# Reading two scalar inputs late instead of first: a one-core attention and gated-MLP kernel on Trainium2

## The chip, the cores and the metric

The kernel runs on one core of one Trainium2 chip, in one launch. The metric is the device time of the whole program in microseconds; it is given as the median of several runs, and less is better.

## What is computed

Attention with a causal window and a few sink positions, and a gated MLP with a spatial mixing step behind it. Cut to what matters (B, H, S, D = 4, 8, 768, 64; d_ff = 1024):

```python
scores = (1 / sqrt(D)) * (q @ k.T)
keep = (pos < n_sink) | ((rel >= 0) & (rel < window))      # n_sink = 4, window = 128
a = exp(where(keep, scores, -1e9) - max); a = a / (a.sum(-1) + 1e-9)
x = a @ v                                                  # heads side by side: (B, 768, 512)
h = relu(x @ w_in); u, v2 = h[..., :512], h[..., 512:]
v_n = (v2 - mean) / sqrt(var + 1e-6)
v_s = w_spatial @ v_n + b_spatial[:, None]
out = (u * v_s) @ w_out
```

`n_sink` and `window` are inputs, two int64 scalars. The kernel holds a fast path that is written for the values 4 and 128, and a general path. The scalars are read and compared with 4 and 128; a branch at the end of the program runs the general path if they differ. Here they don't differ, so the general path is not run.

## The kernel before

The program has five compute engines with a queue of instructions each (TensorE, VectorE, ScalarE, GpSimd, and SyncE, which issues nearly all DMAs). Each queue runs strictly in order. `tile_kernel` (L1199 on) calls `begin` (masks and constants), `read_scalars` (L35), `fast_path` (L462), and then compares the scalars (L1210 to L1215), loads the flag into a register of every engine (`values_load`, L1216) and branches (L1217).

The fast path works on four batches of six tiles of 128 positions, each tile in two halves of four heads. For one half there are score matmuls (`sc`), a masked minimum on VectorE (`pexp`, `nm`, L892), exponentials on ScalarE (L897), transposes of the weights (`tr` on TensorE in the first batch, DMA transposes later), and the product with v (`av`). Then x is transposed (`xT`), and the MLP follows in pieces: `ps_v` (normalised to `vn`), `ps_u` (relu to `u`), `ps_s` (the spatial product with the scaled and split `wsp`, which needs all six chunks of `w_spatial`), and `ps_o`. float32 operands are split into two float16 or float32r parts ("high" on one engine, "low" on another), so the small engines carry many copies and subtractions of 128x512. `w_in` and `w_out` come as 64-bit numbers and are decoded on ScalarE, VectorE and GpSimd (`dec` loads, `w` tiles, L661 to L674).

What sets the order: every piece is added to a `Plan` with a rank, an engine (or several it may run on), an estimated duration and what it reads and writes. `Plan.order` sorts by rank and then runs a list schedule: at each step it picks the piece that can start first by its estimates, so it decides both the order on every queue and, for pieces with several engines, which one runs them. One more piece with an estimated duration can therefore change the order and the engine of other pieces behind it. `FIRST_LOADS` gives the first DMAs of the plan the lowest ranks. What is issued outside the plan, such as `read_scalars`, stands in the program where it is written: ahead of the plan.

The scalar loads before: each of the two DMAs takes one int64 (two int32 words) and writes it into all 128 partitions of the tile `words`, 8 bytes in each. `n_sink` goes through SyncE's queue (q1), `window` through ScalarE's (q10). VectorE turns the words to float (`wf`, L41) and compares.

Of the kernel before, what the change touches and what calls it, by code (L numbers as in the profile page):

```python
# [6 lines left out]
F32 = mybir.dt.float32  # L7
# [3 lines left out]
I32 = mybir.dt.int32  # L11
U32 = mybir.dt.uint32
AF = mybir.ActivationFunctionType
ALU = mybir.AluOpType
AX = mybir.AxisListType
# [4 lines left out]
P = 128  # L20
# [11 lines left out]
EXP_HIGH = bits_as_f32(0x47F00000)  # L32


def read_scalars(tc, pool, n_sink, window):  # L35
    nc = tc.nc
    words = pool.tile([P, 4], I32, name="words")
    nc.sync.dma_start(words[:, 0:2], n_sink.bitcast(I32).partition_broadcast(P))
    nc.scalar.dma_start(words[:, 2:4], window.bitcast(I32).partition_broadcast(P))
    wf = pool.tile([P, 4], F32, name="wf")  # L40
    nc.vector.tensor_copy(wf, words)  # L41
    return words, wf


def f64_to_f32(nc, raw, w, tmp, top=None):
# [231 lines left out]


QUEUED = 3.0
class Plan:  # L280


# [4 lines left out]
    def __init__(self, rings, ring_of):  # L287
        self.pieces, self.rings, self.ring_of = [], rings, ring_of
# [5 lines left out]
    def order(self):  # L294
# [58 lines left out]
        while open_:  # L353
            best = None
            for i in open_:
# [4 lines left out]
                if ps[i][7] and not ps[i][5]:  # L360
                    t = max(t, moved - QUEUED)
                es = ps[i][2] if ps[i][2] not in free else (ps[i][2],)
# [96 lines left out]
    return st  # L459


def fast_path(tc, st, qk, v, v0, vs, w_in, w_sp, b_sp, w_out, out):  # L462

# [1 line left out]
    nc = tc.nc  # L467
    TC = 256
    VNS = 2.0 ** 10
    with (  # L470
# [78 lines left out]
        plan = Plan(rings, dict({k: r for k, (r, _) in makers.items()}, **{r: r for r in rings}))  # L549
# [245 lines left out]
        def load_v(t):  # L795

            k = 2 if t < NV else 1

            def f(e):
                o = v_room[:, t:t + 2] if k > 1 else v_whole(t).unsqueeze(1)  # L800
                nc.sync.dma_start(o, v0[t * P:(t + k) * P, :].rearrange("(c p) f -> p c f", p=P))
            plan.add(early.get(("v", t), 0), "SP", 0.37, f, [], [v_key(t + x) for x in range(k)], dma=0.8 * k)
            if t >= NV:
                j = t - NV
                plan.add(early.get(("v", t), 0), "SP", 0.37, lambda e: nc.sync.dma_start(sinks_whole(j), vs[0, j, :16]), [],
                         [("p16", ("v", j), 1)], dma=0.1)
# [20 lines left out]
        def whole(b):  # L827
            return b < WHOLE
# [331 lines left out]


        W = WHEN
        for t in (0, 2, 4, 5):
            load_v(t)
        w_in_half(1)
# [4 lines left out]
        for i, (b, t, hf) in enumerate(subs):  # L1170
            n = TOGETHER0 if whole(b) else TOGETHER
            for h2 in range(0, HH, n):
                scores(i, b, t, hf, h2, i - W["score"] + h2 * W["pair"], n)
            weights(i, b, t, hf, i - W["split"])
            attend(i, b, t, hf, i)
            if hf == 0:
                queries_keys(b, t, early.get(("q", t), i - W["load"]) if b == 0 else i - W["load"], i - W["qk"])
                if not whole(b):
                    value(b, t, i - W["value"])
                if t == 0:  # L1180
                    v_scale(b, i - W["vscale"])
                continue
            v_half(b, t, i + W["v"])
            if t % 2:
# [17 lines left out]
def tile_kernel(tc, qk, v, v0, vs, n_sink, window, w_in, w_sp, b_sp, w_out, out):  # L1202
    nc = tc.nc
    with tc.tile_pool(name="top", bufs=1) as top:
        with tc.tile_pool(name="first", bufs=1) as pool:
            st = begin(nc, pool)
            words, wf = read_scalars(tc, top, n_sink, window)
            fast_path(tc, st, qk, v, v0, vs, w_in, w_sp, b_sp, w_out, out)
        bad = top.tile([P, 4], F32, name="bad")
        for i, x in enumerate((FAST_N, 0, FAST_W, 0)):  # L1210
            nc.vector.tensor_scalar(bad[:, i:i + 1], wf[:, i:i + 1], float(x), None, op0=ALU.not_equal)
        flag = top.tile([P, 1], F32, name="flag")
        nc.vector.tensor_reduce(out=flag, in_=bad, axis=AX.X, op=ALU.max)
        flagi = top.tile([P, 1], I32, name="flagi")
        nc.vector.tensor_copy(flagi, flag)  # L1215
        rv = nc.values_load(flagi[0:1, 0:1], min_val=0, max_val=1)  # L1216
        with tc.If(rv > 0):  # L1217
            general_path(tc, wf, qk, v, w_in, w_sp, b_sp, w_out, out)

FAST_N, FAST_W = 4, 128  # L1220

# [42 lines left out]
```

## Time and profile before

| what | before |
|---|---|
| median of 3 runs | 443.92 us (441.65 to 444.85) |
| span of the profiled execution | 439.1 us |
| TensorE (PE) busy in it | 414.1 us (94%) |
| VectorE (DVE) busy | 319.1 us (73%) |
| ScalarE (ACT) busy | 272.0 us (62%) |
| GpSimd (POOL) busy | 156.6 us (36%) |
| mean DMA rate | 137 GB/s |

The profiled execution is one run; its span goes from the first to the last recorded instruction, and the measured time is some microseconds more. Stamps below are microseconds from the start of the span. In a row of a timeline, the bracket at the end says how long the engine sat idle before the instruction and what ended that. "PEld" is the loading of TensorE's weights, which overlaps the matmuls.

### The profile page before, as it was taken

How to read it: one execution, taken by the hardware profiler on the slowest of the kernel's cores; microseconds unless marked ns; L12 is line 12 of the kernel's file. 1: busy time of each engine (PE TensorE's matmuls, PEld its weight loads, DVE VectorE, ACT ScalarE, POOL GpSimd, SP SyncE). 2: the span in 40 equal slices, each digit the busy share in tenths (PEclk: the TensorE clock that was granted, in tenths of full speed). 3: DMA queues.
4: the chain of work that ended last, by engine and by line, in shares of the span. 5: the costliest groups of instructions: out<-in, count | busy, mean ns of one | idle time of the engine just before them, and what ended most of it. 6: DMA issues, size and time to landing. Idle time of an engine off the chain costs nothing.

```text
span 439.1 us, 9802 instructions
## 1 busy us (share of the span) xinstructions
PE 414.1 (94%) x3669; PEld 323.9 (74%) x3669; DVE 319.1 (73%) x937; ACT 272.0 (62%) x584; POOL 156.6 (36%) x214
## 2 busy tenths in 40 slices
PE   2689999999989999999999999999999999999994
PEld 1467777777677877877778878868778778688882
DVE  3999988689999885878986966788994645143430
ACT  3898978789977565469864754677664353232211
POOL 4426565645735432238351512343541112000000
PEclk9999999999999999999999999999999999999998
DMA  5999414549976784279964673567723822200011
GB/s 215 384 344 296 119 29 115 169 118 196 175 132 162 182 173 133 41 209 208 189 170 123 134 154 87 73 187 154 135 69 98 137 61 64 73 2 24 25 48 57
DMA packets 117928, 59.98 MB, mean 137 GB/s; under 512 B 100240, under 2 KB 103920, under 8 KB 117872
## 3 DMA queue, kind: packets, MB, share of 16 engines
q1 hardware_dynamic: 117728, 59.27, 55.3%
q8 instruction: 31, 0.51, 0.5%
q14 instruction: 25, 0.20, 0.1%
q10 hardware_dynamic: 144, 0.00, 0.0%
HBM read 28.58 MB, written 6.29 MB: 79 GB/s over the span
## 4 chain that ended last, share of the span: by engine, by line
PE 85%; DVE 9%; DMA 2%; issue 1%; ACT 1%; POOL 0%; SPq 0%; ACTq 0%; DVEq 0%
PE ps_s L608 21%; PE ps_o L608 16%; PE ps_v L608 13%; PE ps_u L608 12%; PE sc L887 6%; PE av L1013 4%; PE sc L881 3%; DVE pexp L892 2%; PE tr L925 2%; PE av L997 1%; PE av L999 1%; PE av L998 1%; DMA qkraw<-qk_t 1%; PE av L1005 1%; DVE wsp L597 1%
## 5 line engine op out<-in xcount | busy, mean ns | idle before, releaser
L608 PE MATMUL ps_s<-wsp,vn 128*128 128x256 f16 x864 | 101.0, 273 | 1.6 <-DVE wsp L597 0.8
L608 PEld LDWEIGHTS <-vn 128*128 128x128 f16 x864 | 82.5, 98 | 14.8 <-issue 2.7
L897 ACT ACTIVATE pexp<-pexp,nm 128x260 f32<-128x260 f32 (+1 forms) x192 | 81.2, 484 | 6.2 <-DVE nm L892 6.0
L608 PE MATMUL ps_o<-wout,g 128*128 128x512 f32 x288 | 70.2, 399 | 0.0
L608 PE MATMUL ps_u<-xT,win 128*128 128x256 f16 x576 | 69.0, 273 | 0.4 <-ACT u L1110 0.4
L608 PE MATMUL ps_v<-win,xT 128*128 128x512 f16 x288 | 66.2, 379 | 1.1 <-ACT u L1110 1.1
L608 PEld LDWEIGHTS ps_o<-wout,g 128*128 128x128 f32 x288 | 53.1, 188 | 12.8
L608 PEld LDWEIGHTS <-win 128*128 128x128 f16 x576 | 54.9, 98 | 10.0 <-issue 1.7
L1131 DVE SCALAR_TENSOR_TENSOR g<-ps_s,isc,b_bc 128x256 f32<-128x256 f32 x48 | 23.1, 481 | 39.6 <-PE ps_s L608 38.2
L608 PEld LDWEIGHTS <-xT 128*128 128x128 f16 x288 | 27.0, 98 | 31.5 <-issue 2.2
L574 ACT CAST g<-g 128x256 fp32r<-128x256 f32 x39 | 15.8, 404 | 50.5 <-DVE g L1135 48.3
L590 DVE TENSOR_TENSOR p<-pexp,p 128x1024 f16<-128x1024 f32 (+2 forms) x56 | 40.6, 747 | 8.6 <-ACT p L574 8.6
L590 POOL TENSOR_TENSOR x<-x,x 128x512 f16<-128x512 f32 x24 | 31.2, 1299 | 22.5 <-ACT x L574 21.4
L887 PE MATMUL sc<-kring,qp 64*128 64x260 f32 (+1 forms) x432 | 35.3, 296 | 0.0
L1110 ACT ACTIVATE u<-ps_u,icu 128x256 f32<-128x256 f32 x48 | 22.3, 469 | 17.2 <-PE ps_u L608 17.2
L887 PEld LDWEIGHTS sc<-kring,qp 64*128 64x128 f32 x432 | 28.1, 186 | 6.3 <-issue 4.2
L1078 POOL TENSOR_TENSOR rs<-rs,mhalf 128x1 f32<-128x1 f32 x24 | 16.2, 676 | 46.0 <-DVE rs L1072 42.5
L1157 ACT COPY ob<-ps_o 128x512 f32<-128x512 f32 x24 | 14.1, 586 | 27.9 <-PE ps_o L608 27.9
L574 ACT CAST p<-pexp 128x32 f16<-128x32 f32 (+2 forms) x52 | 30.7, 620 | 0.5
L1068 DVE BATCH_NORM_STATS2 st<-vr 128x6 f32<-128x512 f32 x24 | 16.5, 689 | 17.2 <-ACT vr L1062 17.2
L590 DVE TENSOR_TENSOR g<-g,g 128x256 fp32r<-128x256 f32 x41 | 22.5, 550 | 8.5 <-ACT g L574 7.9
L997 PE MATMUL av<-vring,pT 128*128 128x65 f16 x264 | 27.7, 193 | 0.0
(143 smaller groups left out, 762.5 us busy)
## 6 DMA issues: line engine op xcount, KB each, us to landing
qkraw<-qk_t SPq DMA_DIRECT2D x18, 512.0 KB, 4.4
out<-ob SPq DMA_DIRECT2D x24, 256.0 KB, 2.3
vraw<-v_s SPq DMA_DIRECT2D x18, 256.0 KB, 4.4
dec<-w_in SPq DMA_DIRECT2D x8, 512.0 KB, 6.9
wsp<-w_sp_t SPq DMA_DIRECT2D x6, 384.0 KB, 6.1
dec<-w_out SPq DMA_DIRECT2D x4, 512.0 KB, 4.5
wsp<-qk_t SPq DMA_DIRECT2D x6, 256.0 KB, 5.5
qkraw<-qk_t SPq DMA_DIRECT2D x6, 256.0 KB, 4.4
```

The lines of the kernel that those rows point to most:

```text
L574: nc.scalar.copy(o, x)
L590: eng[e].tensor_tensor(out=o, in0=x, in1=hi, op=ALU.subtract)
L608: nc.tensor.matmul(o, a, m, start=(i == 0), stop=(i == n - 1))
L887: nc.tensor.matmul(o, qp[rows, qi, hp, :], keys(kring[:, ki], rows), start=(m == 0), stop=(m == 2))
L897: nc.scalar.activation(po, po, AF.Exp, bias=nm()[:, h2 + q:h2 + q + 1], scale=-1.0)
L997: nc.tensor.matmul(o[:, h], ph, vh, start=(t < 2 and j == 0), stop=False)
L1013: nc.tensor.matmul(o[:, h], pT[:, q * P:(q + 1) * P], v_whole(kt)[:, g:g + D + 1], start=(t < 2 and j == 0), stop=(j == nb - 1 and (t < 2 ...
L1068: nc.vector.bn_stats(s6, vr())
L1078: nc.gpsimd.tensor_tensor(out=vals["rs", i], in0=vals["rs", i], in1=mhalf, op=ALU.pow)
L1110: plan.add(r + WHEN["u relu"], "a", 0.36, lambda e: nc.scalar.activation(tl("u", (b, c0))[:, d, :], tl("ps_u", i)[:, :TC], AF.Relu, scale= ...
L1131: nc.vector.scalar_tensor_tensor(out=g(), in0=tl("ps_s", i)[:, :TC], scalar=vals["s", "sp"][1], in1=b_bc[:, t0:t0 + TC], op0=ALU.mult, op1 ...
L1157: plan.add(r + WHEN["o copy"], "a", 0.5, lambda e: nc.scalar.copy(tl("ob", i), tl("ps_o", i)), [("ps_o", i)], [("ob", i)])
```

## The change

The class `Scalars` takes the place of `read_scalars`. Both scalars are now loaded by SyncE, in a piece of the plan with rank 27.0 and an estimated 0.8 us on SyncE, and the seven VectorE instructions of the comparison are a second piece of the same rank, estimated at 1.3 us. Nothing of either stands in front of the plan any more.

```diff
-def read_scalars(tc, pool, n_sink, window):
-    nc = tc.nc
-    words = pool.tile([P, 4], I32, name="words")
-    nc.sync.dma_start(words[:, 0:2], n_sink.bitcast(I32).partition_broadcast(P))
-    nc.scalar.dma_start(words[:, 2:4], window.bitcast(I32).partition_broadcast(P))
-    wf = pool.tile([P, 4], F32, name="wf")
-    nc.vector.tensor_copy(wf, words)
-    return words, wf
+class Scalars:
...
+    def load(self):
+        for i, x in enumerate(self.sources):
+            self.nc.sync.dma_start(self.words[:, 2 * i:2 * i + 2], x.bitcast(I32).partition_broadcast(P))
+
+    def compare(self):
+        v = self.nc.vector
+        v.tensor_copy(self.wf, self.words)
+        for i, x in enumerate((FAST_N, 0, FAST_W, 0)):
+            v.tensor_scalar(self.bad[:, i:i + 1], self.wf[:, i:i + 1], float(x), None, op0=ALU.not_equal)
+        v.tensor_reduce(out=self.flag, in_=self.bad, axis=AX.X, op=ALU.max)
+        v.tensor_copy(self.flagi, self.flag)
...
+SCALARS_AT = 27.0
...
+        plan.add(SCALARS_AT, "SP", 0.8, lambda e: scalars.load(), [], [("words", 0)], dma=0.3)
+        plan.add(SCALARS_AT, "d", 1.3, lambda e: scalars.compare(), [("words", 0)], [("flag", 0)])
...
-            words, wf = read_scalars(tc, top, n_sink, window)
-            fast_path(tc, st, qk, v, v0, vs, w_in, w_sp, b_sp, w_out, out)
...
+            scalars = Scalars(nc, top, n_sink, window)
+            fast_path(tc, st, scalars, qk, v, v0, vs, w_in, w_sp, b_sp, w_out, out)
+        rv = nc.values_load(scalars.flagi[0:1, 0:1], min_val=0, max_val=1)
```

What that does to the queues, at three places. Lines below 462 keep their meaning but move by 15 (L881 becomes L896). First the front of SyncE's queue, the first six rows before (`wsp<-qk_t` is the k of a tile, which in the first batch lies in the room of `wsp`; `qkraw` is its q):

```order
L1260 UNCONDITIONAL_BRANCH
L38 DMA words<-n_sink 128x2
L836 DMA wsp<-qk_t 128x4x128
L602 DMA qkraw<-qk_t 128x512
L602 DMA dec<-w_in 128x1024 x4
L801 DMA vring<-v_ones 128x2x520
```

and of the change:

```order
L1270 UNCONDITIONAL_BRANCH
L851 DMA wsp<-qk_t 128x4x128
L617 DMA qkraw<-qk_t 128x512
L617 DMA dec<-w_in 128x1024 x4
L816 DMA vring<-v_ones 128x2x520
```

The load of `n_sink` has left the front (and that of `window` has left the front of ScalarE's queue). Both stand far behind now, and the flag's load into SyncE's register with them. SyncE before, at the transposes of the first batch's second and third tile:

```order
L719 DMA b_bc<-b_sp 128x768
L1041 DMA_TRANSPOSE xT<-x_576 128x8x128
L602 DMA qkraw<-qk_t 128x512
L1041 DMA_TRANSPOSE xT<-x_756 128x8x128
L602 DMA qkraw<-qk_t 128x2x512
```

and of the change:

```order
L734 DMA b_bc<-b_sp 128x768
L1056 DMA_TRANSPOSE xT<-x_576 128x8x128
L48 DMA words<-n_sink 128x2
L48 DMA words<-window 128x2
L617 DMA qkraw<-qk_t 128x512
L1056 DMA_TRANSPOSE xT<-x_758 128x8x128
L1226 TENSOR_LOAD flagi
L1226 ISA x2
L617 DMA qkraw<-qk_t 128x2x512
```

Before, the register load stood between two `dec` loads near the front. The comparison follows on VectorE. In its queue the low part of the second tile's `vn` has gone to GpSimd at that place. VectorE before:

```order
L1086 TENSOR_SCALAR vr<-vr,mv,rs 128x512
L671 SCALAR_TENSOR_TENSOR w_751<-dec,w_751 128x512
L590 TENSOR_TENSOR vn<-vr,vn 128x512
L892 ISA pexp,nm<-sc,m_even 128x260
L892 ISA nm 128x1
```

and of the change:

```order
L1101 TENSOR_SCALAR vr<-vr,mv,rs 128x512
L686 SCALAR_TENSOR_TENSOR w_753<-dec,w_753 128x512
L52 CAST wf<-words 128x4
L54 TENSOR_SCALAR bad<-wf 128x1 x4
L55 TENSOR_REDUCE flag<-bad 128x1
L56 CAST flagi<-flag 128x1
L907 ISA pexp,nm<-sc,m_even 128x260
L907 ISA nm 128x1
```

Behind this point the planner's picks differ for a while. On TensorE the groups stand in another order from the `ps_v` of the first batch's fourth tile (at 76 us before) up to the first batch's first `ps_s` (at 121 us before); behind that one `ps_v` and one `av` have changed places, and all that follows stands in the same order. VectorE's work on `w_spatial` lies in that stretch. Its last two low parts of `wsp`, which the first `ps_s` needs, before:

```order
L597 SCALAR_TENSOR_TENSOR wsp<-wsp,wsp_scale 128x768
L1022 TENSOR_SCALAR den<-av 128x8
L1023 RECIPROCAL den<-den 128x8
L1024 TENSOR_TENSOR x<-av,den 128x512
L892 ISA pexp,nm<-sc,m_odd 128x260
L892 ISA nm 128x1
L597 SCALAR_TENSOR_TENSOR wsp<-wsp,wsp_scale 128x768
```

and the last one of the change:

```order
L612 SCALAR_TENSOR_TENSOR wsp<-wsp,wsp_scale 128x768
L1037 TENSOR_SCALAR den<-av 128x8
L1038 RECIPROCAL den<-den 128x8
L1039 TENSOR_TENSOR x<-av,den 128x512
L803 TENSOR_TENSOR icv_1789<-v_inv,win_inv 128x1
L907 ISA pexp,nm<-sc,m_odd 128x260
```

The last low part stands ahead of the division of `av` and the mask instructions instead of behind them; the first of the six has moved ahead likewise. On ScalarE the sixth high part of `wsp` has likewise moved ahead of four instructions, the relu that writes `vr`, a small cast of `p`, a scaling of `vring` and a sum over `vraw`.

## Rows read from the trace of the kernel before

**Rows 1.** The head of the page and its part on busy time: microseconds, share of the span, instructions.

```profile
span 439.1 us, 9802 instructions
PE 414.1 (94%) x3669; PEld 323.9 (74%) x3669; DVE 319.1 (73%) x937; ACT 272.0 (62%) x584; POOL 156.6 (36%) x214
```

**Rows 2.** The timeline of TensorE, only the rows that begin after an idle time, in the stretch from 90 to 220 us (behind the last one it has none up to its last matmul): start, duration, engine, line, operation, count, idle time before it.

```profile
102.80 1.47 PE L608 MATMUL ps_u<-xT,win 128*128 128x256 f16 x12 [0.43 <-ACT u L1110]
104.90 0.38 PE L635 MATMUL ps_col<-allmax,ones 1*128 1x1 f32 x2 [0.26 <-DVE allmax L632]
116.99 2.75 PE L608 MATMUL ps_v<-win,xT 128*128 128x512 f16 x12 [1.08 <-ACT u L1110]
123.67 0.27 PE L608 MATMUL ps_s<-wsp,vn 128*128 128x256 f16 x1 [0.53 <-ACT wsp L576]
124.72 2.34 PE L608 MATMUL ps_s<-wsp,vn 128*128 128x256 f16 x20 [0.78 <-DVE wsp L597]
128.18 2.12 PE L608 MATMUL ps_s<-wsp,vn 128*128 128x256 f16 x18 [0.28 <-DVE g L1131]
...
185.55 0.38 PE L635 MATMUL ps_col<-allmax,ones 1*128 1x1 f32 x2 [0.26 <-DVE allmax L632]
```

**Rows 3.** The timeline of all engines in the first 8 us, with the issues of DMAs (SPq, ACTq): start, duration, engine, line.

```profile
0.72 0.39 ACTq L39 DMA_DIRECT2D words<-window  x1
0.72 0.40 SPq L38 DMA_DIRECT2D words<-n_sink  x1
...
1.18 0.67 SPq L836 DMA_DIRECT2D wsp<-qk_t  x1
...
1.90 0.60 SPq L602 DMA_DIRECT2D qkraw<-qk_t  x1
...
5.60 0.17 DVE L41 CAST wf<-words 128x4 f32<-128x4 int32 x1 [4.59 <-DMA words<-n_sink]
...
6.36 0.15 DVE L1215 CAST flagi<-flag 128x1 int32<-128x1 f32 x1
...
7.43 0.98 PE L881 MATMUL sc<-wsp,qkraw 64*128 64x128 f32 x5 [7.43 <-DMA qkraw<-qk_t]
```

**Rows 4.** The view of the DMA queues, issues of the first 5 us: KB each, microseconds from issue to landing.

```profile
wsp<-qk_t SPq DMA_DIRECT2D x1, 256.0 KB, 5.4
qkraw<-qk_t SPq DMA_DIRECT2D x1, 256.0 KB, 5.4
words<-window ACTq DMA_DIRECT2D x1, 1.0 KB, 4.6
words<-n_sink SPq DMA_DIRECT2D x1, 1.0 KB, 4.8
```

**Rows 5.** The same view for the packets between 1.5 and 5.5 us: how many, how many of them small, and by queue (q1 is SyncE's, q10 ScalarE's).

```profile
DMA packets 513, 0.12 MB, mean 29 GB/s; under 512 B 288, under 2 KB 513, under 8 KB 513
...
q1 hardware_dynamic: 369, 0.12, 14.7%
q10 hardware_dynamic: 144, 0.00, 1.6%
```

**Rows 6.** The view by stretches; the last two columns are the mean busy share of the 16 DMA engines and GB/s, the one ahead of them TensorE's granted clock.

```profile
2.50:3.00 0.50, 0.00 (x0) 0.00 (x0) 0.00 (x0) 0.14 (x1) 0.50 (x5) 1.00 0.04 1
4.75:5.00 0.25, 0.00 (x0) 0.00 (x0) 0.00 (x0) 0.00 (x0) 0.00 (x0) 1.00 0.21 13
5.00:5.25 0.25, 0.00 (x0) 0.00 (x0) 0.00 (x0) 0.00 (x0) 0.00 (x0) 1.00 0.45 107
5.50:6.00 0.50, 0.00 (x0) 0.00 (x0) 0.36 (x5) 0.00 (x0) 0.00 (x0) 1.00 1.18 376
50.00:51.00 1.00, 1.00 (x6) 0.66 (x7) 1.00 (x6) 0.97 (x3) 0.85 (x3) 1.00 0.00 0
65.00:66.00 1.00, 1.00 (x10) 0.99 (x9) 1.00 (x8) 1.00 (x4) 1.00 (x1) 1.00 0.29 82
66.00:67.00 1.00, 1.00 (x12) 1.00 (x11) 0.06 (x2) 1.00 (x3) 0.34 (x3) 1.00 0.82 293
```

**Rows 7.** A load that is issued while no other DMA runs: the row of SyncE's timeline, and the row of the view of the DMA queues for 64 to 68.5 us.

```profile
64.52 0.39 SPq L602 DMA_DIRECT2D qkraw<-qk_t  x1
```

```profile
qkraw<-qk_t SPq DMA_DIRECT2D x1, 512.0 KB, 3.5
```

**Rows 8.** The chain of work that ended last, pieces in order of time in its first 40 us: start, duration, what.

```profile
1.90 5.39 DMA qkraw<-qk_t
7.30 0.14 issue
7.43 0.82 PE sc L881 x4
...
21.06 3.98 DMA wsp<-qk_t
```

**Rows 9.** SyncE's timeline where the scalar loads stand in the change, VectorE's and GpSimd's where the comparison stands, and the register load of the flag on SyncE (the view of the tile: duration in ns, start).

```profile
43.68 1.26 SPq L1041 DMA_TRANSPOSE xT<-x  x1
50.02 0.34 SPq L602 DMA_DIRECT2D qkraw<-qk_t  x1
```

```profile
62.08 0.69 DVE L671 SCALAR_TENSOR_TENSOR w<-dec,w 128x512 int32<-128x512 int32 x1
63.12 1.55 DVE L590 TENSOR_TENSOR vn<-vr,vn 128x512 f16<-128x512 f32 x1 [0.35 <-ACT vn L574]
```

```profile
62.85 1.27 POOL L674 TENSOR_TENSOR w<-w,wtmp 128x512 int32<-128x512 int32 x1 [2.32 <-DVE w L671]
```

```profile
L1216 SPq TENSOR_LOAD <-flagi x1: 476/476/476, 15.2 to 15.2; - x1
```

**Rows 10.** The timelines of VectorE and of ScalarE around the last parts of `wsp`, and the stretch from 100 to 150 us in the view by stretches (busy time of PE, PEld, DVE, ACT, POOL).

```profile
122.22 0.15 DVE L1022 TENSOR_SCALAR den<-av 128x8 f32<-128x8 f32 x1
...
123.65 1.02 DVE L597 SCALAR_TENSOR_TENSOR wsp<-wsp,wsp_scale 128x768 f16<-128x768 f32 x1
```

```profile
120.77 0.68 ACT L1062 ACTIVATE vr<-ps_v,icv 128x512 f32<-128x512 f32 x1
...
122.69 0.93 ACT L576 ACTIVATE wsp<-wsp,wsp_scale 128x768 f16<-128x768 f32 x1
```

```profile
100.00:150.00 50.00, 46.63 (x479) 36.22 (x478) 47.01 (x128) 40.98 (x85) 26.04 (x28) 1.00 0.85 175
```

**Rows 11.** VectorE's normal length of such a subtraction, from its timeline at 51 us.

```profile
51.42 0.67 DVE L590 TENSOR_TENSOR vn<-vr,vn 128x512 f16<-128x512 f32 x1
```

More of the change, by code (lines that the diff above doesn't have):

```diff
@@ L32, with __init__ @@
 EXP_HIGH = bits_as_f32(0x47F00000)
-def read_scalars(tc, pool, n_sink, window):
-    nc = tc.nc
-    words = pool.tile([P, 4], I32, name="words")
-    nc.sync.dma_start(words[:, 0:2], n_sink.bitcast(I32).partition_broadcast(P))
-    nc.scalar.dma_start(words[:, 2:4], window.bitcast(I32).partition_broadcast(P))
-    wf = pool.tile([P, 4], F32, name="wf")
-    nc.vector.tensor_copy(wf, words)
-    return words, wf
+class Scalars:
+    def __init__(self, nc, pool, n_sink, window):
+        self.nc, self.sources = nc, (n_sink, window)
+        self.words = pool.tile([P, 4], I32, name="words")
+        self.wf = pool.tile([P, 4], F32, name="wf")
+        self.bad = pool.tile([P, 4], F32, name="bad")
+        self.flag = pool.tile([P, 1], F32, name="flag")
+        self.flagi = pool.tile([P, 1], I32, name="flagi")
+    def load(self):
[8 more added lines that the diff above has]
+        v.tensor_copy(self.flagi, self.flag)
 def f64_to_f32(nc, raw, w, tmp, top=None):
@@ L459, in begin, with fast_path @@
     return st
-def fast_path(tc, st, qk, v, v0, vs, w_in, w_sp, b_sp, w_out, out):
+def fast_path(tc, st, scalars, qk, v, v0, vs, w_in, w_sp, b_sp, w_out, out):
     nc = tc.nc
@@ L1206, in tile_kernel @@
             st = begin(nc, pool)
-            words, wf = read_scalars(tc, top, n_sink, window)
-            fast_path(tc, st, qk, v, v0, vs, w_in, w_sp, b_sp, w_out, out)
[L1209 to L1216, printed above, removed]
+            scalars = Scalars(nc, top, n_sink, window)
+            fast_path(tc, st, scalars, qk, v, v0, vs, w_in, w_sp, b_sp, w_out, out)
+        rv = nc.values_load(scalars.flagi[0:1, 0:1], min_val=0, max_val=1)
         with tc.If(rv > 0):
-            general_path(tc, wf, qk, v, w_in, w_sp, b_sp, w_out, out)
+            general_path(tc, scalars.wf, qk, v, w_in, w_sp, b_sp, w_out, out)
 FAST_N, FAST_W = 4, 128
```

## Prediction

> **What bounds the kernel now.** I read the page first: TensorE is busy 414.1 of 439.1 us [rows 1], so 25 us of its time are idle and the rest can only be gained by less work, which this change doesn't bring. Then I looked for where the idle time lies. TensorE's first matmul starts at 7.43 us [rows 3], with the whole time before it a wait for the first k and q. The timeline shows 3.62 us of waits between 90 and 220 us (0.43, 0.26, 1.08, 0.53, 0.78, 0.28 and 0.26), all but the last of them before 129 us [rows 2]. Most of the rest lies between the first matmul and 40 us, and behind the last one, which the change doesn't touch. So only two places can pay: the front, where everything hangs on the first loads, and the stretch up to 129 us, where the planner's order has changed. Behind that the order on TensorE is the old one and TensorE hardly waits, so what is gained or lost before simply moves the rest.
>
> The chain of waits says what the front hangs on: the load of `qkraw` from 1.90 for 5.39 us, then the score matmuls and VectorE's work on them, and later a load of `wsp` for 3.98 us from 21.06, issued when TensorE has freed its room [rows 8]. Nothing in it is bound to a fixed time. If the first pair of loads lands earlier, the chain moves as a whole.
>
> **The scalars leave the front.** SyncE issues `n_sink` at 0.72 and the first k at 1.18 [rows 3]: 0.46 us of issue is gone in any case. But there is more to see. The k and q land 5.4 us after their issue, twice 256 KB [rows 4], while a single load of 512 KB, issued at 64.52 when no other DMA runs, lands in 3.5 us [rows 7]. The two scalars, 1 KB each, need 4.6 and 4.8 us [rows 4]. Between 1.5 and 5.5 us 513 packets run, of which 288 are under 512 bytes: 144 of q10, which carries nothing but `window`, and as many of q1, whose first piece is `n_sink` [rows 5]. The engines stand nearly idle meanwhile, at 0.04 of their time with 1 GB/s, and the data of the first loads come only from 5.0 us on: 13 GB/s before that, 107 and 376 GB/s behind it [rows 6]. An issue into empty queues isn't that slow to start: for the load of 50.02 us [rows 9] and of 64.52 there is no or little traffic in the first microsecond, and for the second one 293 GB/s between 1.5 and 2.5 us after its issue [rows 6]. I read this as a queue that is held up: the 8-byte writes go through one by one, and the k and q wait behind them.
>
> Without them the k is issued at about 0.72, the q 0.72 us later (1.90 less 1.18) at 1.44, and with the 3.5 us of rows 7 the q is there at 4.94 instead of 7.29 (1.90 + 5.39). That is 2.35 us. **Bounds:** 0.46 us if the slow start belongs to the first DMA of a program, whatever it carries; 3.05 us if the whole stream moves by as much as its start (full rate at 5.25 now, then 0.72 + 1.5 = 2.2). I take 2.35: of the rows that show a start, those at 50 and 64.5 us are nearest to a queue without scalars. The masks are no new bound, since GpSimd stands idle before the k's copy, and VectorE and ScalarE wait for data there.
>
> In the Trainium skill, DMA: Bandwidth & Descriptors, section "Issuing engines are not separate DMA queues", says that DMAs of all issuing engines end up on the same 16 engines; by that `window`, on ScalarE's queue, is a brake like `n_sink`, and the trace agrees with 144 packets of either. The same page, section "Latency and other measured facts", gives some 0.8 us as the least for a tiny transfer; by it the scalars would be gone by about 1.6 us and only the 0.46 us of issue would be won, which is the time of the first rival below. The measured 4.6 and 4.8 us [rows 4] speak against it here.
>
> **The scalars come late.** The two issues take about 0.8 us of SyncE (twice 0.40) behind the transpose of 43.68 (1.26 us). SyncE's next issue is at 50.02 [rows 9], so 5 us of idle time cover them. The words land some 5 us later, at 51; VectorE reaches the comparison at 62.8 (62.08 + 0.69) [rows 9]. The wait is covered by 12 us; without that cover VectorE, with all masks behind it, would stand. The comparison itself took from 5.60 to 6.51 [rows 3], 0.91 us, in a wait; now it takes the place of the low part of `vn`, which stood there with 1.55 us [rows 9]: no loss on VectorE. SyncE's register load now waits for the flag until about 63.7; it took 0.48 us early on [rows 9], and the next load went out at 64.52 [rows 7]. A few tenths at most, for a load that is needed 20 us later. I cost all of this at nothing; the upper end, if VectorE's cover failed, is 0.91 us.
>
> **The order behind it.** TensorE's first `ps_s` waits 0.53 us for ScalarE's and 0.78 us for VectorE's last part of `wsp` [rows 2]. In the changed order VectorE's last part no longer stands behind the division and the first mask (122.22 to 123.65, 1.43 us), nor ScalarE's behind four other instructions (120.77 to 122.69, 1.92 us) [rows 10]. Both leads are longer than the waits, so I take 1.31 us off. The other waits of this stretch (0.43, 0.26, 1.08, 0.28) I keep at their size, though not at their places, since the groups that they stood at have moved. **Bounds:** all six gone, 3.36 us less; or twice as much, 3.36 us more.
>
> **Sum.** 2.35 + 1.31 = 3.66 us: the span goes from 439.1 to 435.4 us. What lies around it, 4.8 us to the median, stays. **443.92 less 3.66 is 440.3 us**, a gain of 0.8%.
>
> **Rivals.**
> *Slow start of any first DMA.* The first k would crawl as the scalars did. For it: the traffic is slow from its first packet, and no other time of the trace starts cold. Against it: 288 small packets are just what runs in that time. Then 443.92 - 0.46 - 1.31 = 442.2 us. Chance 0.22.
> *The waits only move.* The front pays, the order doesn't: another group waits 1.31 us in place of `ps_s`. For it: VectorE is busy 47.01 of 50 us from 100 to 150 [rows 10] and any slip shows. 443.92 - 2.35 = 441.6 us. Chance 0.15.
> *All six waits go.* 443.92 - 2.35 - 3.36 = 438.2 us. Chance 0.07.
> *GpSimd holds up VectorE: slower.* In the new order GpSimd has four large pieces more, the low part of `vn` among them. Where one runs beside a VectorE subtraction, the latter gets longer: 1.55 us at 63.12, beside GpSimd's piece of 62.85 to 64.12 [rows 9], against 0.67 [rows 11], so 0.88 us each. Four such are 3.5 us; VectorE gets rid of about 0.7 us; 2.8 us reach TensorE, as VectorE has only 2.99 us to spare in 50 [rows 10], and the `ps_s` waits stay. 443.92 - 2.35 + 2.8 = 444.4 us. It decides from three such meetings on, where the loss passes 2.35 us. Against it: GpSimd is busy 26.04 of these 50 us, and most of its pieces hurt nobody. Chance 0.06.
> SBUF — State Buffer of the Trainium skill, section "Who interferes with whom", states this as a lock: a VectorE instruction with two SBUF inputs and a GpSimd one that reads SBUF share a port pair, and the later one blocks for the whole of the other. The lengthened row agrees.
>
> **How the numbers follow.** My forecast has a chance of 0.50, with a range of its own of 439.3 to 441.3 us. The range for 8 in 10 reaches over the rivals at 438.2, 441.6 and 442.2 us and up to the slow start without any gain from the order (443.46): 437.8 to 443.5 us. It leaves out the slower rival and the lowest tail. A measurement of this kernel can tell about 1%, 4.4 us, from no change; the forecast lies below that. Faster by over 1% means under 439.5: a fifth of the forecast's half, the 0.07 and a little of the rest, 0.20. Slower by over 1% needs a loss beyond the fourth rival: 0.02. The rest, 0.78, is within 1%.
>
> **What would show it.** Right: TensorE's first matmul at about 5.1 us; k and q landing in about 3.5 us; hardly a packet under 512 bytes before 4 us; no wait at the first `ps_s`; VectorE not waiting for `words`; SyncE's issues behind the flag as before. Wrong: a first matmul near 7.0 us (slow start), new waits of TensorE between 75 and 130 us (the waits move), VectorE subtractions of over 1 us in greater number there (the port). I would be wrong altogether if the gain of the front were lost on the way to 41 us, by a chain that doesn't start with these loads.

## The result, and the profile after

| | before | after |
|---|---|---|
| median of 20 runs each | 442.44 us (440.15 to 445.54) | 446.66 us (443.9 to 451.07) |
| span of the profiled execution | 439.1 us | 446.1 us |
| TensorE's first matmul | 7.43 us | 4.61 us |
| waits of TensorE in the first two `ps_s` groups | 1.31 us | 4.70 us |

The ratio after to before is 1.0097, with an interval of 1.0075 to 1.0119: the change makes the kernel about 1% slower, 4.2 us by the medians. The forecast was 0.8% faster.

The head of the page after, its part on busy time, and TensorE's granted clock in 40 slices of the span:

```profile
span 446.1 us, 9807 instructions
PE 417.3 (94%) x3669; PEld 326.3 (73%) x3669; DVE 323.3 (72%) x934; ACT 270.1 (61%) x583; POOL 160.9 (36%) x218
PEclk9999999989979999999999999999999999999998
```

TensorE is busy 3.2 us longer than in [rows 1] for the same matmuls; the slices with 8 and 7 say where it ran at a lower clock. The first places to look are those of the forecast. The front, from the timeline of all engines (issues of SyncE, the first matmul, ScalarE's first two readings of `dec`, VectorE's first step on `w`, and the `ps_col` that ends the scaling of w_in):

```profile
0.72 0.69 SPq L851 DMA_DIRECT2D wsp<-qk_t  x1
1.47 0.60 SPq L617 DMA_DIRECT2D qkraw<-qk_t  x1
2.12 1.84 SPq L617 DMA_DIRECT2D dec<-w_in  x4
...
4.61 2.71 PE L896 MATMUL sc<-wsp,qkraw 64*128 64x128 f32 x16 [4.61 <-DMA qkraw<-qk_t]
...
9.06 0.66 ACT L678 ACTIVATE w<-dec 128x512 f32<-128x512 f32 x1 [6.84 <-DMA dec<-w_in]
...
9.75 0.69 DVE L676 TENSOR_SCALAR_CACHE_REDUCE w<-w 128x512 f32<-128x512 f32 x1 [3.29 <-ACT w L678]
...
10.75 0.65 ACT L678 ACTIVATE w<-dec 128x512 f32<-128x512 f32 x1
...
18.84 0.58 PE L650 MATMUL ps_col<-allmax,ones 1*128 1x1 f32 x2 [1.06 <-DVE allmax L647]
```

ScalarE's two readings and the `ps_col` in the timeline of before:

```profile
8.60 0.67 ACT L663 ACTIVATE w<-dec 128x512 f32<-128x512 f32 x1 [5.95 <-DMA dec<-w_in]
...
10.31 0.67 ACT L663 ACTIVATE w<-dec 128x512 f32<-128x512 f32 x1
...
18.38 0.58 PE L635 MATMUL ps_col<-allmax,ones 1*128 1x1 f32 x2 [0.99 <-DVE allmax L632]
```

The first matmul comes 2.82 us earlier than in [rows 3], and 14 us later the gain is gone: `ps_col` is 0.46 us late. In between stands the decoding of w_in, whose first load ScalarE reads at 9.06 instead of 8.60 us; VectorE, done with its first masks, stands 3.29 us for it. The view by stretches says how fast the loads came, after:

```profile
2.00:3.00 1.00, 0.00 (x0) 0.00 (x0) 0.00 (x0) 0.21 (x2) 1.00 (x7) 1.00 0.59 166
3.00:4.00 1.00, 0.00 (x0) 0.00 (x0) 0.00 (x0) 0.00 (x0) 1.00 (x10) 1.00 1.22 378
4.00:5.00 1.00, 0.39 (x4) 0.42 (x6) 0.00 (x0) 0.00 (x0) 0.97 (x8) 1.00 0.66 168
...
7.00:8.00 1.00, 0.32 (x3) 0.02 (x1) 0.00 (x0) 0.00 (x0) 0.00 (x0) 1.00 0.93 229
```

and before, for the stretches in which its stream ran:

```profile
5.00:6.00 1.00, 0.00 (x0) 0.00 (x0) 0.36 (x5) 0.00 (x0) 0.00 (x0) 1.00 0.96 293
6.00:7.00 1.00, 0.00 (x0) 0.00 (x0) 0.45 (x5) 0.00 (x0) 0.29 (x3) 1.00 1.10 430
7.00:8.00 1.00, 0.57 (x5) 0.60 (x6) 0.00 (x0) 0.00 (x0) 0.51 (x4) 1.00 0.99 393
```

After, the stream starts 3 us earlier and then falls to 168 and 229 GB/s, with the DMA engines busy for 0.66 and 0.93 of the time, against 0.99 at 393 GB/s. The last column of the view is GB/s, which for stretches of 1 us is also KB: between 2 and 9 us it is 1.80 MB after (166, 378, 168, 315, 274, 229, 274) against 1.55 MB before (1, 5, 7, 293, 430, 393, 422). A lead of 0.25 MB at 410 GB/s is 0.6 us, not 2.8.

The rate isn't all of it, since the first `dec` lands later although more has come by then (1.8 MB by 9 us, against 1.4 MB by 8.6 us before). The trace holds 16 landing stamps for every load, which no view prints, and ScalarE's reading follows the last of them. Before, those of the first `dec` lie between 8.22 and 8.57 us. After, 14 of them lie between 5.63 and 6.67 us, and the last two at 8.18 and 9.04. So most of the load comes nearly 2 us earlier, and its last parts don't.

The second place is the first `ps_s` groups. The rows of TensorE's timeline from 90 to 220 us that begin after an idle time, to be read against [rows 2]:

```profile
101.53 1.47 PE L623 MATMUL ps_u<-xT,win 128*128 128x256 f16 x12 [0.67 <-ACT vr L1077]
106.73 2.75 PE L623 MATMUL ps_v<-win,xT 128*128 128x512 f16 x12 [0.34 <-DVE allmax_r L654]
127.73 0.38 PE L623 MATMUL ps_s<-wsp,vn 128*128 128x256 f16 x2 [2.80 <-DVE wsp L612]
130.01 4.00 PE L623 MATMUL ps_s<-wsp,vn 128*128 128x256 f16 x18 [1.90 <-ACT vr L1077]
```

Two waits of 2.80 and 1.90 us stand where 0.53 and 0.78 stood, and the second group, of 18 matmuls, takes 4.00 us where [rows 2] have 2.12 for as many. The granted clock in the stretch (third number from the right, ahead of the DMA share and GB/s):

```profile
125.00:130.00 5.00, 0.38 (x2) 0.19 (x2) 4.93 (x13) 1.52 (x4) 1.21 (x1) 0.83 0.69 161
130.00:135.00 5.00, 4.99 (x37) 3.79 (x37) 3.74 (x11) 3.56 (x9) 2.62 (x3) 0.50 0.23 52
```

It was 1.00 before [rows 10]; now TensorE is idle for 4.62 of 5 us, and then runs at 0.50 of its 2.4 GHz. The scores ahead of `ps_s` start at 122.09 us, 1.69 us later than the 120.40 of before; the matmuls behind the second group start at 133.81, 6.91 later than 126.90. Of the 7.0 us between the two spans, 5.2 (6.91 less 1.69) arise here, and the 3.39 us more of waits (4.70 less 1.31) and 1.88 us more for the slow group (4.00 less 2.12) account for them. The timelines of VectorE, ScalarE and GpSimd show what was late:

```profile
124.22 2.54 DVE L612 SCALAR_TENSOR_TENSOR vring<-vraw,v_scale,vring 128x512 f16<-128x512 f32 x1
126.68 1.00 DVE L612 SCALAR_TENSOR_TENSOR wsp<-wsp,wsp_scale 128x768 f16<-128x768 f32 x1
...
128.03 0.69 DVE L1039 TENSOR_TENSOR x<-av,den 128x512 f32<-128x512 f32 x1
128.64 0.15 DVE L803 TENSOR_TENSOR icv<-v_inv,win_inv 128x1 f32<-128x1 f32 x1
```

```profile
128.76 0.62 ACT L589 CAST x<-x 128x512 f16<-128x512 f32 x1 [3.48 <-DVE x L1039]
129.28 0.68 ACT L1077 ACTIVATE vr<-ps_v,icv 128x512 f32<-128x512 f32 x1
```

```profile
123.78 2.43 POOL L605 TENSOR_TENSOR p<-pexp,p 128x1024 f16<-128x1024 f32 x1 [2.18 <-ACT p L589]
```

VectorE's last part of `wsp` stands behind a `vring` part of 2.54 us, which took 0.74 before; it ran while GpSimd subtracted `p`. And `vr`, which empties the PSUM bank of the last `ps_v`, now stands on ScalarE behind the cast of `x`, which waits for VectorE's division, which waits behind that last `wsp` part. Before, `vr` ran at 120.77 [rows 10]. `ps_v`, `ps_u`, `ps_s` and `ps_o` share two banks (`BANKS["mm"]`): the first `ps_s` group has one, and the second must wait for the other.

### The profile page after: what moved, and what is told of

Its sections match the earlier page's. It is cut to its first block, busy times and chain, and to the rows that moved or that the text cites. A ratio compares the mean times of both kernels' runs of the same rounds, so it can differ in the third digit from the quotient of the medians.

```text
span 446.1 us, 9807 instructions
## 1 busy us (share of the span) xinstructions
PE 417.3 (94%) x3669; PEld 326.3 (73%) x3669; DVE 323.3 (72%) x934; ACT 270.1 (61%) x583; POOL 160.9 (36%) x218
## 4 chain that ended last, share of the span: by engine, by line
PE 86%; DVE 6%; DMA 4%; ACT 2%; issue 1%; SPq 1%; ACTq 0%
PE ps_s L623 21%; PE ps_o L623 15%; PE ps_v L623 14%; PE ps_u L623 13%; PE sc L902 7%; PE av L1028 4%; PE sc L896 3%; DMA dec<-w_in 2%; PE tr L940 2%; PE av L1012 2%; PE av L1013 2%; PE av L1014 2%; PE av L1020 1%; DMA wsp<-qk_t 1%; DVE pexp L907 1%
## 5 line engine op out<-in xcount | busy, mean ns | idle before, releaser
L623 PE MATMUL ps_s<-wsp,vn 128*128 128x256 f16 x864 | 102.9, 276 | 4.7 <-DVE wsp L612 2.8
L623 PEld LDWEIGHTS <-vn 128*128 128x128 f16 x864 | 83.4, 99 | 18.5 <-issue 5.8
L623 PE MATMUL ps_u<-xT,win 128*128 128x256 f16 x576 | 69.9, 275 | 0.7 <-ACT vr L1077 0.7
L1146 DVE SCALAR_TENSOR_TENSOR g<-ps_s,isc,b_bc 128x256 f32<-128x256 f32 x48 | 23.1, 481 | 40.7 <-PE ps_s L623 39.2
L605 DVE TENSOR_TENSOR p<-pexp,p 128x1024 f16<-128x1024 f32 (+2 forms) x56 | 41.7, 769 | 6.2 <-ACT p L589 6.2
L1125 ACT ACTIVATE u<-ps_u,icu 128x256 f32<-128x256 f32 x48 | 22.5, 471 | 20.9 <-PE ps_u L623 20.7
L605 DVE TENSOR_TENSOR g<-g,g 128x256 fp32r<-128x256 f32 x41 | 23.9, 584 | 8.5 <-ACT g L589 7.9
L589 ACT CAST p<-pexp 128x32 f16<-128x32 f32 (+2 forms) x50 | 28.7, 603 | 0.5
```

The lines of the kernel that those rows point to most:

```text
L589: nc.scalar.copy(o, x)
L605: eng[e].tensor_tensor(out=o, in0=x, in1=hi, op=ALU.subtract)
L623: nc.tensor.matmul(o, a, m, start=(i == 0), stop=(i == n - 1))
L1125: plan.add(r + WHEN["u relu"], "a", 0.36, lambda e: nc.scalar.activation(tl("u", (b, c0))[:, d, :], tl("ps_u", i)[:, :TC], AF.Relu, scale= ...
L1146: nc.vector.scalar_tensor_tensor(out=g(), in0=tl("ps_s", i)[:, :TC], scalar=vals["s", "sp"][1], in1=b_bc[:, t0:t0 + TC], op0=ALU.mult, op1 ...
```

## The experiments

Theory A: the loss comes from the changed order of the other work, and the gain of the front is lost before 41 us. Theory B: the late loads and the late comparison cost it themselves. The first two runs split the change.

**Late scalars, old order.** The plan is made without the two scalar pieces, which are then put back after as many instructions of SyncE and VectorE as in the change.

```diff
...
+        places = []
+        for own, on in ((f_load, "SP"), (f_compare, "d")):
+            at = [f for f, e in full].index(own)
+            places.append((own, on, sum(e == on for f, e in full[:at])))
+        plan.pieces = [p for p in plan.pieces if p[4] not in (f_load, f_compare)]
+        order = plan.order()
+        for own, on, n in places:
+            at = [i for i, (f, e) in enumerate(order) if e == on][n]
+            order.insert(at, (own, on))
```

> The scalars are loaded and compared late, as in the change, but every other instruction stands in the order of the kernel before. Theory A (the loss comes from the changed order of the other work, and the gain of the front is lost before 41 us because the decoding of w_in bounds the front): first matmul at about 4.6 us, first ps_s waits about 1.3 us in all as before, time within 0.3% of the kernel before (ratio 0.997 to 1.003). My recorded front term, if it reached the end: 2.35 us less, ratio 0.995. Theory B (the late loads and the late comparison themselves cost the time): ratio 1.007 or more.

Measured: 441.84 against 441.66 us, ratio 0.9985 (0.9958 to 1.0012); first matmul at 4.73 us. Theory B falls. The waits at `ps_s`, in TensorE's timeline, are nearly those of [rows 2]:

```profile
126.29 0.27 PE L623 MATMUL ps_s<-wsp,vn 128*128 128x256 f16 x1 [0.65 <-ACT wsp L591]
127.35 2.34 PE L623 MATMUL ps_s<-wsp,vn 128*128 128x256 f16 x20 [0.78 <-DVE wsp L612]
```

The front's 2.35 us (ratio 0.995) lie outside the interval: 1.9 us at most (0.42%) came through, and nothing is within it. By the two medians the run is no faster at all.

**Early scalars, new order.** The counterpart: the scalars are loaded and compared early, as before, and two empty pieces stand in the plan in their place.

```diff
-        plan.add(SCALARS_AT, "SP", 0.8, lambda e: scalars.load(), [], [("words", 0)], dma=0.3)
-        plan.add(SCALARS_AT, "d", 1.3, lambda e: scalars.compare(), [("words", 0)], [("flag", 0)])
+        plan.add(SCALARS_AT, "SP", 0.8, lambda e: None, [], [("words", 0)], dma=0.3)
+        plan.add(SCALARS_AT, "d", 1.3, lambda e: None, [("words", 0)], [("flag", 0)])
...
+            scalars.load()
             fast_path(tc, st, scalars, qk, v, v0, vs, w_in, w_sp, b_sp, w_out, out)
+        scalars.compare()
...
```

> The scalars are loaded in front and compared early, as in the kernel before, but two empty pieces in the plan give all other instructions the order of the change. Theory A (order): first matmul at about 7.4 us as before, the first ps_s wait over 3 us in all, ratio 1.008 to 1.012 to the kernel before. Theory B (the late loads themselves): ratio 1.000 to 1.003.

Measured: 447.07 us, ratio 1.0127 (1.0081 to 1.0173). Two pieces that issue nothing cost as much as the whole change, a little more than I expected. TensorE's timeline has the same two waits and the same slow group, now with a first matmul at 7.38 us:

```profile
126.91 0.38 PE L624 MATMUL ps_s<-wsp,vn 128*128 128x256 f16 x2 [2.81 <-DVE wsp L613]
129.19 4.00 PE L624 MATMUL ps_s<-wsp,vn 128*128 128x256 f16 x18 [1.90 <-ACT vr L1078]
```

**Two instructions put back.** On the change, `icv` goes behind `v_inv`, and `vr` behind ScalarE's last `wsp` part. Here and below, `behind` moves the first of two pieces, each named by its engine and by what it writes, to the place right behind the second.

```diff
...
+        behind(("d", ("icv", 1)), ("d", ("scale", ("v", 1))))
+        behind(("a", ("vr", (1, 0))), ("a", ("wsp", 5, 0), ("wspraw", 4)))
```

> The change, with two instructions of its order put back: icv of the second batch directly behind v_inv on VectorE, and the vr that reads it behind the last wsp part on ScalarE, ahead of the cast of x. Theory A: the second wait of the first ps_s group (1.90 us for ScalarE's vr in the profile of the change) goes, with a part of the low clock behind it (ps_s x18 took 4.00 us there); 2 to 4 us less than the change, ratio 1.001 to 1.005 to the kernel before. Rival (the wait only changes its releaser, since TensorE then stands for something else): as the change, ratio 1.008 to 1.012.

Measured: 442.64 us, ratio 1.0022 (0.9995 to 1.005). The change's 1.0097 shrinks by 0.75%, 3.3 us, for two moved instructions, and the two intervals don't overlap. In TensorE's timeline the second wait is gone, the first one stands, and a low clock follows it:

```profile
124.92 3.92 PE L623 MATMUL ps_s<-wsp,vn 128*128 128x256 f16 x20 [2.81 <-DVE wsp L612]
129.52 2.13 PE L623 MATMUL ps_s<-wsp,vn 128*128 128x256 f16 x18
```

From the scores ahead of `ps_s` to the matmuls behind the second group TensorE takes 9.42 us here, 11.72 in the change and 6.50 before. So the profiles show 2.3 of the 3.3 us at this place; the rest is no larger than the intervals.

**Which of the two?** Only `icv` put back.

```diff
...
+        behind(("d", ("icv", 1)), ("d", ("scale", ("v", 1))))
```

> The change, with icv of the second batch put back behind v_inv on VectorE, and nothing else. If ScalarE's place of vr, behind the cast of x, is what holds the second ps_s group: the wait stays at about 1.9 us and names ScalarE's vr. Rival (icv on VectorE, behind the division, is what holds it): the wait goes below 0.5 us.

Measured in a single run: span 444.1 us, waits of 2.77 and 1.90 us, the second still for ScalarE's `vr`, which starts at 128.86 behind the cast of `x` at 128.33. So an early `icv` alone doesn't free the second group; what holds it is the place of `vr` on ScalarE's queue.

**The meeting with GpSimd taken away.** On the run with two instructions put back, the `p` subtraction goes from GpSimd to VectorE, behind the division (`at` finds the place of a piece).

```diff
...
+        low17 = order.pop(at("p", ("p16", 17, 1)))[0]
+        order.insert(at("d", ("x", (1, 1))) + 1, (low17, "d"))
```

> As the run before it, and the subtraction p of 128x1024 that GpSimd ran beside VectorE's vring part is given to VectorE, behind its division x. Theory A (that meeting made vring 2.54 instead of 0.74 us and so the last wsp part late): vring takes about 0.75 us, the first wait of the first ps_s shrinks from 2.80 to about 1.0 us, 1.8 us less than the run before it, ratio 0.997 to 1.002. Rival (VectorE, which has 1.1 us more to do, gives it back at the next masks): the same time as the run before it.

Measured: 444.21 us, ratio 1.0049 (1.002 to 1.0078), not faster than the run without this step; the two intervals overlap. In the profiled execution (438.2 us) the place itself did what was expected: `vring` took 0.74 us and the wait shrank to 1.00. But TensorE then waited for VectorE's `g`:

```profile
122.41 2.34 PE L623 MATMUL ps_s<-wsp,vn 128*128 128x256 f16 x20 [1.00 <-DVE wsp L612]
126.37 2.13 PE L623 MATMUL ps_s<-wsp,vn 128*128 128x256 f16 x18 [0.78 <-DVE g L1146]
133.31 2.75 PE L623 MATMUL ps_v<-win,xT 128*128 128x512 f16 x12 [1.82 <-DVE g L1146]
```

So the cause of the long `vring` is shown. The two new waits, 2.60 us, are more than the 1.81 us that the first one lost, as the rival had it: VectorE gives the gain back. Why the median is above this execution, the fastest of its 12 runs, no row shows.

**My order term alone.** On the late scalars with the old order, the last `wsp` parts come earlier by hand.

```diff
...
+        behind(("d", ("vslot0", (1, 2), 1)), ("d", ("wsp", 4, 1), ("wspraw", 3)))
+        behind(("a", ("wsp", 5, 0), ("wspraw", 4)), ("d", ("wsp", 4, 1), ("wspraw", 3)))
+        behind(("d", ("wsp", 5, 1), ("wspraw", 4)), ("d", ("vslot0", (1, 2), 1)))
```

> The kernel with late scalars and the old order, in which the last parts of wsp come earlier by hand: ScalarE's ahead of its vring and junk, VectorE's ahead of the division and the first mask, VectorE's vring part behind the one before. This is my recorded order term alone. If it holds: the waits of the first ps_s (0.65 and 0.78 us in the run with the old order) go or shrink below 0.3 us in all, 1.3 us less than that run, ratio 0.994 to 0.997 to the kernel before. Rival (the waits only move to the groups that need the delayed mask and division): ratio 0.997 to 1.001, with new waits of TensorE of about 1 us before 150 us.

Measured: 443.72 against 442.15 us, ratio 1.0035 (1.0 to 1.0071), above both ranges that I expected. ScalarE's wait is gone, VectorE's stays, and the second group now stands 2.18 us for VectorE's `g`:

```profile
125.21 2.34 PE L623 MATMUL ps_s<-wsp,vn 128*128 128x256 f16 x20 [0.79 <-DVE wsp L612]
130.58 2.93 PE L623 MATMUL ps_s<-wsp,vn 128*128 128x256 f16 x18 [2.18 <-DVE g L1146]
```

VectorE reaches that `g` at 130.05 us, behind the division, four masks, statistics and a `p`, later against TensorE by the part that was drawn forward. That `p` met GpSimd: it took 1.62 us, beside a subtraction of GpSimd from 128.04 to 130.10, and the next one of its size took 0.16. Even without the planner's other moves, this arrangement doesn't give my 1.31 us.

**What the front hangs on.** In the first run of two, the four `dec` loads are issued ahead of the k and q; in the second, ScalarE issues them from the start.

```diff
...
+        sp = [i for i, (f, e) in enumerate(order) if e == "SP"][:6]
+        for n, i in enumerate(sp[2:]):
+            order.insert(n, order.pop(i))
```

> The kernel with late scalars and the old order, and on SyncE's queue the four dec loads of w_in ahead of the first k and q. Theory A (the front ends with ps_col, which hangs on the decoding of w_in; the k and q only have to be there in time): first matmul at about 8 us, yet the first dec read by ScalarE at about 5.5 us instead of 8.1 (two loads of 256 KB, 1.3 us, and their issue no longer ahead of it), ps_col 1 to 2 us earlier than 17.9 us, ratio 0.994 to 0.998 to the kernel before. Rival, my recorded step (the chain of k and q moves the front as a whole): the first matmul 3 us later and everything behind it too, ratio 1.003 to 1.006.

```diff
...
+        sp = [i for i, (f, e) in enumerate(order) if e == "SP"][:6]
+        for n, i in enumerate(sp[2:]):
+            order.insert(n, (order.pop(i)[0], "a"))
```

> The kernel with late scalars and the old order, and the first four dec loads issued by ScalarE from the start, beside SyncE's k and q. Theory A: the dec loads no longer stand 1.4 us of issue behind the k and q; the first dec is read at about 6 to 7 us, the first matmul comes at 5 to 7 us, ps_col 1 us earlier than 17.9 us, ratio 0.995 to 0.999. Rival (the 16 DMA engines are the bound between 3 and 9 us, whoever issues): first dec no earlier than 7.5 us, ratio 0.998 to 1.002.

Measured: ratios 1.0067 (1.0035 to 1.0098) and 1.0069 (1.0039 to 1.0098). Both expectations of theory A were wrong. The first `dec` is read early, at 4.30 and 4.55 us, but the k and q land behind those 2 MB or among them, the first matmul is at 11.35 and 10.13 us, and ScalarE's second reading of `dec`, which stands behind the first exponentials on its queue, only at 13.21 and 11.98. `ps_col` comes at 22.21 and 20.97 us. So the front needs both: neither the k and q nor w_in alone sets its end.

**Small scalars.** On the kernel before, the scalars go to one partition, 2 packets instead of 256. The first version leaves the other partitions at zero; in the second the path that isn't taken loads its own limits.

```diff
-    nc.sync.dma_start(words[:, 0:2], n_sink.bitcast(I32).partition_broadcast(P))
-    nc.scalar.dma_start(words[:, 2:4], window.bitcast(I32).partition_broadcast(P))
+    nc.sync.dma_start(words[:, 0:2], n_sink.bitcast(I32).partition_broadcast(n))
+    nc.scalar.dma_start(words[:, 2:4], window.bitcast(I32).partition_broadcast(n))
...
```

The cut is from the second version; `n` is 1 where the scalars are loaded early.

> The kernel before, its scalars loaded early as before, but into one partition only (2 packets of 8 bytes instead of 256; the other partitions are set to zero, so the path that this input doesn't take would lack its limits). If the 8-byte packets hold up the queue, as I recorded: first matmul at 4.9 to 5.5 us, two small packets before 3 us. Rival (the first DMA of a program starts slowly, whatever it carries): 7 us.

> The kernel before with its order and its early loads, but the scalars go to one partition (2 packets of 8 bytes in place of 256) and are compared there; the path that this input doesn't take loads its limits for all partitions itself, so nothing is left out. First matmul at 4.8 to 5.9 us. If the front is set by the second of the w_in decodings (ps_col follows ScalarE's second reading of dec by 7.7 to 8.1 us in every run so far): ps_col at 16.5 to 19 us, anywhere within what the loads give, ratio 0.994 to 1.000, most likely 0.997. My recorded step (the front moves as a whole by over 2 us): ratio 0.994 to 0.995.

Measured: the first version, in a single run, has its first matmul at 5.86 us (k issued ahead of `n_sink` here), `ps_col` at 16.77 and a span of 438.3. The second has 5.14 and 18.14 us, and over 12 runs a ratio of 1.0011 (0.9977 to 1.0045), where I expected 1.000 at most. The packets do hold up the first loads, and taking them away gains nothing at the end.

**The stream.** Why does it slow down? In the first of two runs nothing but `dec` is issued behind the k and q until the first `dec` is decoded.

```diff
...
+        dec = [i for i in sp if str(keys.get(id(order[i][0]))).startswith("(('dec', ('in'")]
+        for n, i in enumerate(dec[4:6]):
+            order.insert(sp[6] + n, order.pop(i))
```

> The kernel with late scalars and the old order, with the fifth and sixth dec load issued before the later loads of the front (vring, the second k and q, p); the sixth has to wait until the first dec is decoded, so nothing else is issued until then. The time of the kernel is of no interest here, but what the queue carries between 4 and 9 us. Theory S (a stream that starts early is slow for its first microseconds, whatever is issued behind it): 140 to 350 GB/s from 4 to 9 us as in the other runs with late scalars, ScalarE's second dec at 9.5 us or later. Rival (the issues of the later loads slow the stream down): about 400 GB/s from 4 us on, second dec at 9 us or earlier.

Measured: 188, 246, 250, 201 and 242 GB/s from 4 to 9 us, second `dec` at 11.64. In this single run the later issues aren't what slows it. In the second, the first k waits for VectorE.

```diff
...
+                    if i == (0, 0):
+                        for c in range(5):
+                            nc.vector.memset(st.wout.bitcast(F32)[:, c // 4, c % 4, :], 0.0)
+                        nc.vector.memset(room[:, :, 2:4], 0.0)
...
```

> The kernel with late scalars and the old order, whose first k waits for VectorE to clear a little of its room, which it does only behind 2560 elements of other clearing, so that the first loads are issued at 3 to 4.5 us and no small packet runs before them. Theory S (slow for its first microseconds, whenever it starts): under 350 GB/s for the 4 us that follow the first full microsecond, ps_col 1 to 3 us later than in the run with the old order. Rival (it is slow until some 8 us after the program's start, and fast afterwards, as the kernel before shows, whose stream starts at 5 us): about 400 GB/s from the second microsecond of the stream on, ps_col at 17.5 to 19 us.

Measured: issue at 3.76 us, `ps_col` at 20.15, span 443.1. The view by stretches:

```profile
6.00:7.00 1.00, 0.00 (x0) 0.00 (x0) 0.00 (x0) 0.00 (x0) 0.00 (x0) 1.00 1.11 386
7.00:8.00 1.00, 0.18 (x2) 0.21 (x4) 0.00 (x0) 0.00 (x0) 0.77 (x5) 1.00 0.98 295
...
9.00:10.00 1.00, 0.95 (x9) 0.91 (x8) 0.67 (x8) 0.40 (x1) 0.00 (x0) 1.00 1.01 233
10.00:11.00 1.00, 0.52 (x5) 0.23 (x3) 0.69 (x2) 1.00 (x3) 0.00 (x0) 1.00 0.92 246
```

At 9 to 11 us, where the kernel before has over 400 GB/s, this stream is slow: the slow microseconds go with the start of the stream and not with the time. Started as late as before, but without the scalars ahead of it, it ends the front 1.8 us later than before (20.15 against 18.38). One more thing differs: its `dec` loads are issued from 5.15 us on, while the data run, and before they were all issued by 4.62 us, ahead of nearly all data. No run tells the packets from the earlier issue.

No run is faster than the kernel before by more than its interval; the late scalars with the old order, at a ratio of 0.9985, come nearest.

## Why the prediction was wrong

**The front, 2.35 us: the mechanism was right, the last clause was not.** The q landed at 4.5 us (1.47 and 3.0), and the first matmul came at 4.61 where I had 5.1. "If the first pair of loads lands earlier, the chain moves as a whole" is the sentence that failed. I took it from the chain of waits, which shows the one path that ended last; the decoding of w_in ran beside it and was ready at the same time: before, VectorE's masks ended at 9.28 us and ScalarE's first `w` at 9.27 (8.60 and 0.67). In eleven profiles with the same queue order (before, after and nine runs), `ps_col` starts 7.7 to 8.1 us behind ScalarE's second reading of `dec`: 10.31 to 18.38 before, 10.75 to 18.84 after, 9.80 to 17.88 with late scalars and the old order, 12.09 to 20.15 with the held start. That reading waits for the loads of w_in. Before, their stream was at full rate and their parts landed together; when it starts at once, the rate is lower and the last parts stray. How far they stray differs between executions. In the six profiles with the front of the change `ps_col` comes at 17.16, 17.63, 17.88, 18.74, 18.84 and 19.31 us, and in the two with the scalars in 128 partitions ahead at 18.38 and 18.32. The 0.46 us that the profile after loses are one draw; on the whole the front gains next to nothing. I had named the loss "on the way to 41 us, by a chain that doesn't start with these loads" as what would make me wrong altogether, and gave it no chance of its own.

**The late scalars cost nothing: right.** They land at about 50 us (46.07 and 3.7), VectorE compares at 63.87 without a wait, and the next load goes out at 65.70, later than before only by the lag that TensorE has by then (1.18 us). The run with the old order bounds it, together with the front: 0.9985, 1.0012 at most.

**The order, 1.31 us: the sign was wrong.** The step "both leads are longer than the waits, so I take 1.31 us off" looked at what stands between the last `wsp` parts and the instructions that I knew, and took their durations from before. What the profiles showed in its place is +3.4 us of waits and +1.9 us of clock, and the order alone costs 1.3% (early scalars, new order). The part ahead of the last one took 2.54 instead of 0.74 us beside GpSimd; and behind the first group, ScalarE's `vr` had been put behind the cast of `x`, so that the wait for the last `wsp` part was handed on through the division and the cast to the second group. I didn't ask who frees the banks of the second group. The lead alone was too little as well: with `vring` at 0.74 us again, the first wait was still 1.00 us. And the experiment on my term alone failed without all this, at VectorE's `g`.

**The rivals.** The waits did move, which I priced as an exchange of 1.31 us; they grew to 4.70 us. The meeting with GpSimd, which I gave 0.06 and "from three such meetings on" (by its own numbers, 0.88 us each less 0.7, it takes four), counted with a single one of 1.80 us, since it stood ahead of the part for which TensorE was waiting. It wasn't what decided: with it in place, but `vr` put back, the loss is down to 0.22%, and its interval reaches down to 0.9995. SBUF — State Buffer of the Trainium skill, section "Who interferes with whom", has the later of two such pieces block for the whole of the other; the trace agrees, with `vring` ending 0.55 us behind GpSimd's `p` (126.76 and 126.21), and with 0.74 us for it once `p` had moved. My bound for the order, 3.36 us the other way, was the size of the added waits (3.39 us) but left out the clock behind them (1.88 us), and I gave that side no part of the range.

**What isn't settled.** Of the profiled 7.0 us, 1.7 lie ahead of 122 us: 0.46 from the front and, at 94 to 98 us, a low clock (below). The low clock there stands in the profile of the early scalars with the new order too (0.50 from 94 to 96 us), so it may belong to this order; the cause is open. Why the stream starts slowly, and why it doesn't with a crawl of small packets ahead, is shown as a fact and not explained.

## What to carry to other kernels

A small piece in a list scheduler's plan isn't small: it can change the order of everything behind it, and two empty pieces cost 1.3% here. For each group of matmuls behind a wait ask two things of the new order, what brings its inputs and what frees its PSUM bank, and follow the second through the in-order queue of the engine that frees it. A gain at the start of a front is worth only what the slowest of its parallel chains gains, so find how far behind the next chain is before you book it.

## What the runs showed of the hardware

The loads' rate at their start: between 110 and 350 GB/s in nearly every microsecond of the 4 to 5 us behind the first full one, in all twelve profiles without the 256 small packets (the largest exception is one stretch of 404); 393 to 431 GB/s from 6 to 11 us in the two that had them ahead. The 16 landing stamps of the first w_in load lie within 0.35 and 0.27 us of each other in these two, and 0.8 to 4.1 us apart in the other twelve.

TensorE's clock fell to half behind the waits at `ps_s` (0.83 and 0.50 in the stretches shown). In the Trainium skill, TensorE: Matmul & The Clock Gate, section "HAM oscillation — how this bites in real kernels", waits between groups of matmuls throw the clock back to 1.2 GHz. The trace agrees there, but the clock also fell without any idle time. In the profile after:

```profile
92.00:94.00 2.00, 2.00 (x17) 1.69 (x16) 1.15 (x6) 2.00 (x7) 0.52 (x1) 1.00 0.61 135
94.00:96.00 2.00, 2.00 (x16) 1.67 (x16) 1.58 (x4) 1.65 (x4) 0.47 (x2) 0.54 0.72 236
96.00:98.00 2.00, 2.00 (x13) 1.49 (x11) 1.97 (x3) 0.00 (x0) 1.92 (x2) 0.60 0.65 158
```

TensorE was busy throughout from 84 us on. It cost 1.5 us: the score group of 12 there took 1.67 and the `ps_u` behind it 2.32 us, against 1.00 and 1.49 in the run with `icv` alone put back, which has the same order on TensorE and no such fall.

The granted clock doesn't tell all: in the profile of the late scalars with the old order TensorE's 16 `av` matmuls at 32.83 us took 3.67 us, against 2.00 in the same group of before, at 33.00 us, both with a granted clock of 1.00. That execution had its first `ps_col` half a microsecond earlier than before (17.88), and the one ahead of its first `ps_v` 2.5 us later (43.42 against 40.91). In twelve of the fourteen profiles 22.5 to 23.1 us lie between these two, in this one 25.5 and in the run with only `dec` behind the k and q 26.9, where the same 16 matmuls took 3.67 us as well. What ends the half rate no row shows, and it can hide a gain of the front in a single execution.
